# A gated attention and two feed-forward layers on one core: values loaded without padding, low weight parts of the first block on GpSimd, tiles 7 to 9 in three terms

## The chip, the core and the metric

One core of a Trainium2 chip runs the whole program. The time is device microseconds of one execution, and shorter is better. The kernel before takes 883.21 us (median of 3 runs, 882.9 to 884.86).

## What is computed

A gated linear attention over 4 batches, 8 heads, 768 tokens and 48 dimensions per head, whose output (3072 tokens of 384 values) goes through two feed-forward layers of width 2048:

```python
f = 1.0 / (1.0 + np.exp(-f_logit))
for t in range(S):
    state = f[:, :, t, :, None] * state + np.einsum('bhd,bhe->bhde', k[:, :, t], v[:, :, t])
    y[:, :, t] = np.einsum('bhd,bhde->bhe', q[:, :, t], state)
x = y.transpose(0, 2, 1, 3).reshape(B * S, H * D)
h = np.maximum(x @ w_in, 0.0);  x = h * h @ w_out            # first layer
h = x @ w_in2;  x = np.where(h > 0, h, np.exp(np.minimum(h, 0)) - 1) @ w_out2   # second layer
```

The weights are float64 in memory and q, k, v and the gates float32.

## The kernel before

The tokens are cut into 24 **chunks** of 128 (numbered g; one batch each, so chunks 0 to 3 begin the four batches), and four chunks make one **block** of 512 tokens. There are six blocks in the first layer and six in the second. A layer has 16 **weight tiles** f, each with an up half (384 to 128) and a down half (128 to 384). One pair (block, tile) is a **unit**; unit u's up product `ph` (line 475) stands in TensorE's queue ahead of the down product `y` (line 539) of unit u-2, and attention work of later chunks is set between them by the table `plan`, filled with `at(slot, f, ...)`: what is planned for slot u is written ahead of the up product of unit u.

A product of the first layer comes in two forms. **Three-term** splits both operands into a high part (rounded to fp32r) and a low part (the remainder) and adds high by high, low by high and high by low, three fp32r instructions per 128x128 block of weights. **One-term** multiplies fp32 as it is, two passes per block of weights. In block 0 the up products of tiles 0 to 2 (`DIRECT` = 3) and the down products of tiles 0 to 9 (`WHOLE` = 10) are one-term, everything else is three-term.

In block 0 the weights have to be made first. `load_raw` fetches the float64 tile; `begin_weights` (ScalarE, two instructions, lines 71 and 73) and `finish_weights` (VectorE, two instructions, lines 81 and 82) turn it into fp32 in a tile called `pair` or `dec`; `store_weights` allocates the lasting tile `w0_f` and, for a one-term tile, has a DMA copy the raw fp32 half into it; `split_up` makes the high part on ScalarE (line 435) and the low part on VectorE (line 436), of the up half alone where f < `WHOLE`, of both halves from there on. `split_rest` does the remaining halves in block 1. Tile f is begun at slot f-3, finished at f-2, split at f-1 and used by `up` at slot f. `between` evacuates `ph`: square of the ReLU, and for a three-term down product also the rounded `gh` (VectorE, line 502) and the remainder `gl` (VectorE in block 0, line 516; GpSimd later, line 522).

Per chunk VectorE runs `a_decay` (two scans, lines 182 and 184), `a_scale` (k and q times the decays, line 204), `a_mask` (two predicated copies out of PSUM, line 260) and `a_states` (lines 248 to 251); GpSimd runs half of the gate (`ff`, line 174), a small product `wc` (line 191) and a small copy into `ends` (line 194).

The opening, before slot 2, is a list written out by hand: `START`, one letter and number per step (f, q, v: loads; r: `load_raw`; g, d, c, s, t, k, m, y, x: attention of chunks 0 to 3; b, w, C, S: begin, finish, store, split; U, B: up and between). All loads go through SyncE's queue, in which each DMA also waits for the DMA eight places ahead of it. Values of chunks 0 to 3 come padded from memory: 128x672 (`vz`) instead of 128x384 (`vk`), so that the output of a head pair lands in the right rows.

Engines run their queues in order, and the order of all of it is the order in which the program writes it.

Of the kernel before, what the change touches and what calls it, by code (L numbers as in the profile page):

```python
# [11 lines left out]
F32 = mybir.dt.float32  # L12
# [5 lines left out]
AF = mybir.ActivationFunctionType  # L18
# [13 lines left out]
BLOCKS = [(layer, sum(n[:i]), n[i]) for layer, n in enumerate(SIZES) for i in range(len(n))]  # L32


START = """f0 f1 q0 I q1 M f2 v0 f3 v1 g0 q2 d0 q3 c0 g1 r0 d1 s0 W v2 c1 v3 t0 g2 k0 m0 g3 r1 s1 t1 y0 d2 c2
x0 r2 k1 m1 s2 d3 f4 q4 t2 y1 c3 b0 k2 s3 m2 x1 r3 t3 b1 y2 x2 m3 y3 x3 w0 k3 r4 b2 w1 U0 C0 r5 b3 w2 B0 h0 h1 w3 g4 h2 h3
f5 l0 l1 C1 U1 l2 l3 r6 C3 S3 B1 C2 T"""
STAGED = 27
DIRECT = 3
EARLY = 14  # L40
WHOLE = 10
NEAR = dict(zip(range(B, NG), (5, 8, 10, 12, 19, 21, 23, 25, *range(28, 4 * NG - 23, 4))))
ORDER = np.r_[64:128, 63:-1:-1]
DMIN = 2.0**-52
# [3 lines left out]
def at_(p, j):  # L48

    return j  # L50
# [31 lines left out]
    V.scalar_tensor_tensor(out=out, in0=hi, scalar=0x80000000, in1=out, op0=ALU.bitwise_and, op1=ALU.bitwise_or)  # L82


def chunked(ctx, tc, ff, qk, vk, vz, wraw, mask, ident, flag, out):

# [50 lines left out]
    def load_qk(g):  # L139
# [5 lines left out]
        else:  # L145
# [2 lines left out]
            nc.sync.dma_start(out=s["k"], in_=qk[g, :, 1])  # L148
            nc.sync.dma_start(out=s["q"], in_=qk[g, :, 0])

    def load_v(g):
        if g < B:

            if g % 2 == 0:
                t = two.tile([128, 2, NK, 2, 112], F32, tag=f"x{'hl'[g // 2]}", name=f"vz{g}")
                st["vz"] = t
            v = st["vz"][:, g % 2]
            nc.sync.dma_start(out=v.rearrange("r k j d -> r (k j d)"), in_=vz[g])
            st.setdefault(g, {})["vz"] = v
            return  # L160
        v = two.tile([128, NP, 2, 48], F32, tag="vk", name=f"vk{g}")
# [100 lines left out]
    def a_state(g):  # L262
        s = st[g]
        kvp = ps_a.tile([128, NP, 48], F32, tag="a0", name=f"kv{g}")
        for p in range(NP):
            for j, (lo, hi) in enumerate(((0, 64), (64, ROWS))):
                v = s["vz"][:, p, at_(p, j), 0:48] if p < NK else s["vz"][:, :, at_(p, j), 96:112]
                PE.matmul(kvp[lo:hi, p], s["kt"][:, p, lo:hi], v, start=True, stop=True)
        A.activation(state[g % B], kvp[:ROWS], AF.Copy)

    def a_direct(g):
# [67 lines left out]
    def a_whole(g):  # L339

        if g == 0:
            st["x"] = wpool.tile([128, NK, 512], F32, tag="w", name="x")
        A.activation(st["x"][:, :, 128 * g:128 * g + 128], st[g]["yp"], AF.Copy)

    def a_hi(g):
        i, o = where[g]
# [39 lines left out]
        raws[layer, f] = raw = pool.tile([128, 2 * DM], I64, tag=tag, name=f"raw{layer}_{f}")  # L386
        nc.sync.dma_start(out=raw, in_=wraw[layer, f])

    decs = {}

    def begin_weights(f):

# [7 lines left out]
        decs[f] = b  # L400

    def finish_weights(f):
        finish(nc, raws.pop((0, f)), decs[f])

    def store_weights(f):

        wt[0, f] = t = wpool.tile([128, 2, 2, DM], F32R, tag="w", name=f"w0_{f}")
        if f >= WHOLE:
            return
        t, b = t.bitcast(F32), decs[f].bitcast(F32)  # L410
        if f < DIRECT:
            nc.sync.dma_start(out=t[:, 1].rearrange("r i m -> r (i m)"), in_=b)
        else:
            nc.sync.dma_start(out=t[:, 1, 1], in_=b[:, DM:])

    def split_up(f):
        b = decs.pop(f).bitcast(F32)
        if f < WHOLE:
            split(wt[0, f][:, :, 0:1], b[:, :DM])
        else:  # L420
            split(wt[0, f], b)

    def split_rest(f):
        t = wt[0, f] if f < DIRECT else wt[0, f][:, :, 1:2]
# [101 lines left out]
    def down(i, f):  # L526
        layer, t0, n = BLOCKS[i]
        gh, gl, gg = hs.pop((i, f))
        if gh is None:
            terms = (wt[0, f][:, 1, 1].bitcast(F32), gg),  # L530
        else:
            w = wt[layer, f]
            terms = (w[:, 0, 1], gh), (w[:, 1, 1], gh), (w[:, 0, 1], gl)
        if f == 0:
            yp_[i] = [ps_y.tile([128, n], F32, tag=f"y{m}", name=f"y{i}_{m}") for m in range(NK)]
        for c in pieces(i, f):
            for m in range(NK):
                for n_, (w, b) in enumerate(terms):
                    PE.matmul(  # L539
                        yp_[i][m][:, c], w[:, 128 * m:128 * m + 128], b[:, c],  # L540
                        start=(f == 0 and n_ == 0), stop=(f == NF - 1 and n_ == len(terms) - 1),
                        skip_group_check=i == final[0],
                    )
            if f == NF - 1:
                dst = out if layer else x2d
                for m in range(NK):
                    if c.start == 0:
                        yo[m] = three.tile([128, n], F32, tag="yo", name=f"yo{i}_{m}")
                    y = yo[m][:, c]
                    if m % 2 == ((i, f) != final):  # L550
                        A.activation(y, yp_[i][m][:, c], AF.Copy)  # L551
                    else:
                        V.tensor_copy(y, yp_[i][m][:, c])
                    ends = (i, f) == final and m == NK - 1 and c.stop == n
                    (nc.scalar if ends else nc.sync).dma_start(out=dst[m, :, t0 + c.start:t0 + c.stop], in_=y)
# [61 lines left out]
    with tc.manual_schedule():  # L617
        V.memset(lim, DMIN)
        V.memset(ends[:, B], 1.0)
        V.memset(ss[0], 0.0)  # L620
        G.memset(ss[1], 0.0)
        for a in sd:
            G.memset(a, 0.0)

        def busy():
            again = ps_a.tile([128, 512], F32, tag="a1", name="busy")
            for _ in range(2):
                PE.matmul(again, idt, idt.unsqueeze(1).to_broadcast([128, 4, 128]), start=True, stop=True)

        warm = ps_a.tile([128, 512], F32, tag="a2", name="warm")  # L630
        for _ in range(3):
            PE.matmul(warm, ss[0][:, 0, 0], ss[0][:, 0].rearrange("r p t -> r (p t)"), start=True, stop=True)
        steps = {
            "I": lambda: nc.sync.dma_start(out=idt, in_=ident),
            "M": lambda: nc.sync.dma_start(out=msk, in_=mask),
            "T": lambda: [nc.sync.dma_start(out=tri[c:c + 64], in_=mask[c:c + 64, 64 - c:128 - c]) for c in (0, 64)],
            "f": load_f, "q": load_qk, "v": load_v, "r": lambda f: load_raw(0, f),
            "g": a_gate, "d": a_decay, "c": a_scale, "s": a_scores, "t": a_transposed, "m": a_mask, "k": a_state,
            "y": a_direct, "h": a_hi, "l": a_lo,
            "x": a_whole, "b": begin_weights, "w": finish_weights, "C": store_weights, "S": split_up, "W": busy,  # L640
            "U": lambda f: up(0, f), "B": lambda f: between(0, f),
            "L": lambda f: low(0, f),
        }
# [120 lines left out]


def _layout(q, k, v, f_logit, moe_w_in, moe_w_out, moe2_w_in, moe2_w_out):
# [14 lines left out]
    vz = np.zeros((B, 128, NK, 2, 112), v.dtype)
    vp = vk[:B].reshape(B, 128, NP, 2, D)
    for kk in range(NK):
        for j in range(2):
            vz[:, :, kk, j, :48] = vp[:, :, kk, at_(kk, j)]
            vz[:, :, kk, j, 96:] = vp[:, :, NK, at_(NK, j), 16 * kk:16 * kk + 16]
    vz = vz.reshape(B, 128, -1)
# [13 lines left out]
    for c, a in enumerate((f_logit, q, k, v)):  # L801
# [20 lines left out]
```

## Time and profile before

| | us |
|---|---|
| median of 3 runs | 883.21 |
| profiled execution | 885.04 |
| its span, first to last instruction | 883.2 |
| TensorE busy in the span | 868.0 |
| VectorE busy | 555.7 |
| ScalarE busy | 454.5 |
| GpSimd busy | 280.3 |

The page gives each engine's busy time; the chain of work that ended last is 94% TensorE. Inside the span the load changes by stage: up to about 37 us the opening, with DMAs at their limit; to about 110 us block 0 of the first layer, where the weights are made; then the blocks that only use them. So what the change does is read in the first 110 us. In a timeline row the columns are start, duration, engine, line, operation, output and input, shape, count, and in brackets how long the engine stood idle ahead of it and what ended that.

### The profile page before, as it was taken

The numbers are of one execution on the slowest core, as the hardware profiler recorded it, in microseconds if no ns is written. First come the engines' busy times: TensorE is split into PE (matmuls) and PEld (weight loads), VectorE is DVE, ScalarE is ACT, GpSimd is POOL, SyncE is SP. The second block draws the span as 40 slices with busy tenths as digits, with TensorE's granted clock in tenths as the row PEclk, the third lists the DMA queues.
The fourth block names the chain that finished last, engine by engine and source line by source line (L and its number), as shares of the span: only waits on it lengthen the run. The fifth ranks groups of instructions, "written<-read, shape, count | busy, mean of one in ns | idle before, by whom it ended". The sixth has DMA issues, their size and how long they took to land.

```text
span 883.2 us, 16000 instructions
## 1 busy us (share of the span) xinstructions
PE 868.0 (98%) x6262; PEld 701.1 (79%) x6262; DVE 555.7 (63%) x841; ACT 454.5 (51%) x812; POOL 280.3 (32%) x248
## 2 busy tenths in 40 slices
PE   7999999999999999999999999999999999999996
PEld 4566788888888888888888888888888888888885
DVE  8899796876778777644331655655654664564543
ACT  4778845555445555454554544544444444544443
POOL 2121065423333333323232333233332322322331
PEclk9999999999999999999999999999999999999998
DMA  8994232235434434422776300100100101000001
GB/s 268 345 301 138 57 108 87 84 115 184 153 121 151 151 117 152 150 77 107 252 275 224 131 13 1 66 6 11 62 1 27 46 1 39 33 1 37 1 1 39
DMA packets 35779, 91.22 MB, mean 103 GB/s; under 512 B 5728, under 2 KB 12352, under 8 KB 35696
## 3 DMA queue, kind: packets, MB, share of 16 engines
q1 hardware_dynamic: 35552, 90.00, 30.6%
q8 instruction: 50, 0.82, 0.4%
q14 instruction: 33, 0.27, 0.1%
q10 hardware_dynamic: 144, 0.13, 0.0%
HBM read 64.55 MB, written 22.02 MB: 98 GB/s over the span
## 4 chain that ended last, share of the span: by engine, by line
PE 94%; DMA 3%; DVE 1%; ACT 1%; SPq 0%; issue 0%; ACTq 0%; DVEq 0%
PE y L539 44%; PE ph L475 44%; DMA raw<-wraw 3%; PE o L294 1%; PE o L309 1%; PE tp L210 1%; PE sk_a L233 1%; DMA q<-qk 1%; PE sk_a L242 1%; PE sk_h L242 0%; PE sk_h L233 0%; DVE t L508 0%; SPq L136 0%; DVE xl L356 0%; DVE pair L81 0%
## 5 line engine op out<-in xcount | busy, mean ns | idle before, releaser
L522 POOL TENSOR_TENSOR gl<-gg,gh 128x512 fp32r<-128x512 f32 x175 | 234.5, 1340 | 452.6 <-PE ph L475 192.1
L539 PE MATMUL y<-gh,wf 128*128 128x512 f32 (+1 forms) x582 | 177.9, 387 | 0.3 <-ACT yo L551 0.3
L508 DVE SCALAR_TENSOR_TENSOR t<-r,t 128x512 f32<-128x512 f32 (+1 forms) x97 | 72.3, 745 | 154.6 <-ACT r L507 154.4
L539 PE MATMUL y<-gh,w 128*128 128x512 f32 x516 | 158.9, 389 | 0.0
L504 ACT ACTIVATE r<-ph 128x512 f32<-128x512 f32 (+1 forms) x97 | 57.8, 596 | 181.3 <-PE ph L475 176.4
L475 PE MATMUL ph<-xh,w 128*128 128x512 f32 x558 | 148.0, 400 | 0.0
L475 PE MATMUL ph<-xh,wf 128*128 128x512 f32 (+1 forms) x582 | 146.4, 387 | 0.0
L539 PEld LDWEIGHTS y<-gh,wf 128*128 128x128 f32 x582 | 108.8, 188 | 22.7 <-ACT yo L551 0.5
L475 PEld LDWEIGHTS ph<-xh,wf 128*128 128x128 f32 x582 | 108.6, 188 | 22.3
L475 PEld LDWEIGHTS ph<-xh,w 128*128 128x128 f32 x558 | 101.3, 188 | 22.1 <-issue 0.5
L539 PEld LDWEIGHTS y<-gh,w 128*128 128x128 f32 x516 | 96.9, 188 | 20.1
L539 PE MATMUL y<-gl,wf 128*128 128x512 f32 (+1 forms) x291 | 112.6, 387 | 0.0
L496 ACT ACTIVATE r<-ph 128x512 f32<-128x512 f32 x86 | 51.3, 596 | 104.2 <-PE ph L475 88.9
L539 PE MATMUL y<-gl,w 128*128 128x512 f32 x258 | 100.4, 389 | 0.0
L475 PE MATMUL ph<-xl,wf 128*128 128x512 f32 (+1 forms) x291 | 81.0, 387 | 0.0
L475 PE MATMUL ph<-xl,w 128*128 128x512 f32 x279 | 78.5, 390 | 0.0
L502 DVE TENSOR_TENSOR gh<-r 128x512 fp32r<-128x512 f32 x68 | 47.1, 693 | 44.4 <-ACT r L496 44.3
L509 DVE SCALAR_TENSOR_TENSOR gg<-ph,t 128x512 f32<-128x512 f32 (+1 forms) x97 | 66.6, 686 | 10.4 <-DVE t L508 0.5
L539 PEld LDWEIGHTS y<-gl,wf 128*128 128x128 f32 x291 | 54.6, 188 | 11.2
L475 PEld LDWEIGHTS ph<-xl,wf 128*128 128x128 f32 x291 | 54.3, 188 | 11.1
L506 ACT ACTIVATE t<-r 128x512 f32<-128x512 f32 (+1 forms) x97 | 61.1, 630 | 3.1
L507 ACT ACTIVATE r<-r 128x512 f32<-128x512 f32 (+1 forms) x97 | 61.0, 629 | 3.1
(112 smaller groups left out, 1027.2 us busy)
## 6 DMA issues: line engine op xcount, KB each, us to landing
raw<-wraw SPq DMA_DIRECT2D x32, 768.0 KB, 7.0
wst<-w SPq DMA_DIRECT2D x16, 768.0 KB, 3.3
wf<-wst SPq DMA_DIRECT2D x16, 768.0 KB, 4.7
k<-qk SPq DMA_DIRECT2D x22, 224.0 KB, 3.5
q<-qk SPq DMA_DIRECT2D x22, 224.0 KB, 4.6
ff<-ff SPq DMA_DIRECT2D x21, 227.9 KB, 6.6
x2d<-yo SPq DMA_DIRECT2D x18, 256.0 KB, 2.8
x<-x2d SPq DMA_DIRECT2D x18, 256.0 KB, 3.0
```

What stands on the lines that cost most here:

```text
L210: PE.transpose(tp[:, p, 0:ROWS], k[:, p], idt[:ROWS, :ROWS])
L233: PE.matmul(sc[j][64 * c:64 * c + 64, p], k[lo:hi, p, 64 * c:64 * c + 64], q[lo:hi, p, 64 - 64 * c:128 - 64 * c], start=True, stop=True,)
L475: PE.matmul(ph, w[:, a, 0, 128 * k:128 * k + 128], b[:, k, c], start=(m == 0), stop=(m == len(todo) - 1))
L496: A.activation(r[:, c], ph, AF.Relu)
L502: V.tensor_tensor(out=gh[:, c], in0=r[:, c], in1=r[:, c], op=ALU.mult)
L504: A.activation(r[:, c], ph, AF.Relu, scale=-1.0)
L506: A.activation(t[:, c], r[:, c], AF.Tanh, scale=-0.5)
L507: A.activation(r[:, c], r[:, c], AF.Exp, scale=-1.0)
L508: V.scalar_tensor_tensor(out=t[:, c], in0=r[:, c], scalar=1.0, in1=t[:, c], op0=ALU.add, op1=ALU.mult)
L509: V.scalar_tensor_tensor(out=gg[:, c], in0=ph, scalar=0.0, in1=t[:, c], op0=ALU.max, op1=ALU.add)
L522: G.tensor_tensor(out=gl, in0=gg, in1=gh, op=ALU.subtract)
L539: PE.matmul(yp_[i][m][:, c], w[:, 128 * m:128 * m + 128], b[:, c], start=(f == 0 and n_ == 0), stop=(f == NF - 1 and n_ == len(terms) - 1) ...
```

## The change

- Values of chunks 0 to 3 are loaded as 128x384 like all others. `kv` (line 268) reads them directly; a new step `a_padded` (letter z) copies them on ScalarE, two instructions per chunk, into padded tiles whose gaps GpSimd zeroes once, for the product `yp`.
- In `START`, `f4`, `r4`, `q4` and others stand elsewhere: the raw tiles 3 and 4 are loaded ahead of k and q of chunk 4, and the gate of chunk 4 comes last.
- The fp32 weights of tile 0 are finished in halves, and the last quarter of x is copied in three pieces.
- The one-term down products of tiles 0 to 2 read the fp32 `pair` tile instead of the copy that the DMA makes.
- `split_up` makes high and low part one half at a time, and the low part on GpSimd for tiles 4 to 15; tile 3 stays on VectorE.
- `WHOLE` goes from 10 to 7: the down products of tiles 7 to 9 in block 0 become three-term. They need `gh` and `gl`, their down halves are split at once, and their raw copies and their `split_rest` fall away.

```diff
-x0 r2 k1 m1 s2 d3 f4 q4 t2 y1 c3 b0 k2 s3 m2 x1 r3 t3 b1 y2 x2 m3 y3 x3 w0 k3 r4 b2 w1 U0 C0 r5 b3 w2 B0 h0 h1 w3 g4 h2 h3
-f5 l0 l1 C1 U1 l2 l3 r6 C3 S3 B1 C2 T"""
+x0 r2 k1 m1 s2 d3 t2 z2 y1 c3 b0 z3 k2 s3 m2 x1 r3 f4 r4 q4 t3 b1 y2 x2 m3 y3 x3 w0 k3 b2 w1 U0 r5 b3 C0 w2 U1 B0 h0 h1 w3 C1 h2 h3
+f5 r6 l0 l1 C3 S3 l2 l3 B1 g4 C2 T"""
...
-WHOLE = 10
+WHOLE = 7
...
+    def a_padded(g):
+        v, z = st[g]["vk"], padded[g // 2][:, g % 2]
+        A.activation(z[:, :, :, 0:48], v[:, :NK], AF.Copy)
+        A.activation(z[:, :, :, 96:112], v[:, NK].rearrange("r j (k d) -> r k j d", k=NK), AF.Copy)
+        st[g]["vz"] = z
...
-        A.activation(st["x"][:, :, 128 * g:128 * g + 128], st[g]["yp"], AF.Copy)
+        for k in [slice(k, k + 1) for k in range(NK)] if g == B - 1 else [slice(0, NK)]:
+            A.activation(st["x"][:, k, 128 * g:128 * g + 128], st[g]["yp"][:, k], AF.Copy)
...
-        finish(nc, raws.pop((0, f)), decs[f])
+        raw = raws.pop((0, f))
+        for c in (slice(0, DM), slice(DM, 2 * DM)) if f == 0 else (slice(0, 2 * DM),):
+            finish(nc, raw[:, c], decs[f][:, c])
...
     def split_up(f):
         b = decs.pop(f).bitcast(F32)
-        if f < WHOLE:
-            split(wt[0, f][:, :, 0:1], b[:, :DM])
-        else:
-            split(wt[0, f], b)
+        t = wt[0, f]
+        for i in range(1 if f < WHOLE else 2):
+            A.activation(t[:, 0, i], b[:, DM * i:DM * i + DM], AF.Copy)
+        for i in range(1 if f < WHOLE else 2):
+            E = G if f > DIRECT else V
+            E.tensor_tensor(out=t[:, 1, i], in0=b[:, DM * i:DM * i + DM], in1=t[:, 0, i], op=ALU.subtract)
```

The first place is GpSimd's queue in block 0. `ff` is the gate, `wc` and `ends` belong to a chunk's decays, `w0_f` is the lasting weight tile f. Before:

```order
L174 TENSOR_SCALAR ff6_530<-ff6_530 112x521
L191 TENSOR_TENSOR wc6_674<-ds0_90,ends_88 112x4
L194 COPY ends_88<-ds0_90 112x8
L174 TENSOR_SCALAR ff7_634<-ff7_634 112x521
L191 TENSOR_TENSOR wc7_841<-ds1_91,ends_88 112x4
L194 COPY ends_88<-ds1_91 112x8
```

and now:

```order
L180 TENSOR_SCALAR ff6_548<-ff6_548 112x521
L432 TENSOR_TENSOR w0_7_654<-pair6_509,w0_7_654 128x384 x2
L197 TENSOR_TENSOR wc6_693<-ds0_90,ends_88 112x4
L200 COPY ends_88<-ds0_90 112x8
L432 TENSOR_TENSOR w0_8_697<-pair8_624,w0_8_697 128x384 x2
L180 TENSOR_SCALAR ff7_652<-ff7_652 112x521
L432 TENSOR_TENSOR w0_9_819<-pair8_624,w0_9_819 128x384 x2
L197 TENSOR_TENSOR wc7_870<-ds1_91,ends_88 112x4
L200 COPY ends_88<-ds1_91 112x8
L432 TENSOR_TENSOR w0_10_874<-pair10_704,w0_10_874 128x384 x2
L432 TENSOR_TENSOR w0_11_996<-pair10_704,w0_11_996 128x384 x2
```

The low parts of tiles 4 to 15 now stand in this queue (one instruction each for tiles 4 to 6, two each for 7 to 15), that of tile 10 behind `wc7` and `ends7`; in the same way that of tile 4 stands behind the gate `ff5` and that of tile 5 behind `ends5`.

The second place is VectorE's queue around tile 9, before (`pair` tiles are weights being finished, `sd`, `s0`, `s1` and `state` belong to a chunk's states):

```order
L436 TENSOR_TENSOR w0_8_678<-pair8_606,w0_8_678 128x384
L81 SCALAR_TENSOR_TENSOR pair8_606<-pair8_606,raw0_9_511 128x768
L82 SCALAR_TENSOR_TENSOR pair8_606<-raw0_9_511,pair8_606 128x768
L260 COPY_PREDICATED sd1_96<-tri_92,sk5_a2_727 128x256
L260 COPY_PREDICATED sd1_96<-tri_92,sk5_h_728 128x256
L248 TENSOR_TENSOR s0_97<-state1_100,wc5_524 112x192
```

and now:

```order
L81 SCALAR_TENSOR_TENSOR pair8_624<-pair8_624,raw0_9_529 128x768
L82 SCALAR_TENSOR_TENSOR pair8_624<-raw0_9_529,pair8_624 128x768
L513 TENSOR_TENSOR gh0_7_720<-r0_7_722 128x512
L527 TENSOR_TENSOR gl0_7_721<-gg0_7_723,gh0_7_720 128x512
L266 COPY_PREDICATED sd1_96<-tri_92,sk5_a2_751 128x256
L266 COPY_PREDICATED sd1_96<-tri_92,sk5_h_752 128x256
L254 TENSOR_TENSOR s0_97<-state1_100,wc5_542 112x192
```

A low part leaves VectorE's queue per tile (tiles 4 to 15), and `gh` and `gl` of tiles 7, 8 and 9 enter it.

The third place is SyncE's queue in the opening, before:

```order
L387 DMA raw0_1_206<-wraw 128x768
L387 DMA raw0_2_247<-wraw 128x768
L136 DMA ff4_281<-ff 112x521
L148 DMA k4_284<-qk 112x512
L149 DMA q4_283<-qk 112x512
L387 DMA raw0_3_335<-wraw 128x768
L387 DMA raw0_4_383<-wraw 128x768
```

and now:

```order
L393 DMA raw0_1_214<-wraw 128x768
L393 DMA raw0_2_257<-wraw 128x768
L393 DMA raw0_3_343<-wraw 128x768
L136 DMA ff4_345<-ff 112x521
L393 DMA raw0_4_347<-wraw 128x768
L148 DMA k4_350<-qk 112x512
L149 DMA q4_349<-qk 112x512
```

Raw tile 3 moved ahead of three loads of chunk 4.

## Rows read from the trace of the kernel before

**Rows 1.** Stretches: length, busy us (count) by engine, granted clock, DMA share, GB/s.
```profile
20.00:30.00 10.00, 8.51 (x118) 6.65 (x115) 8.99 (x12) 6.93 (x12) 0.00 (x0) 1.00 1.04 336
...
36.00:110.00 74.00, 73.92 (x748) 49.68 (x747) 65.97 (x105) 60.60 (x111) 11.08 (x13) 1.00 0.59 187
```

**Rows 2.** Timeline of TensorE at the end of the opening.
```profile
34.36 2.84 PE L464 MATMUL ph<-x,pair 128*128 128x512 f32 x6 [1.24 <-ACT r L484]
37.28 2.84 PE L539 MATMUL y<-gg,w 128*128 128x512 f32 x6
```

**Rows 3.** Timeline of ScalarE there: raw tile 3 has landed.
```profile
32.16 0.90 ACT L71 ACTIVATE pair<-raw 128x768 f32<-128x768 f32 x1 [2.56 <-DMA raw<-wraw]
```

**Rows 4.** Timeline of VectorE there.
```profile
24.18 1.36 DVE L260 COPY_PREDICATED ss<-msk,sc 128x512 f32<-128x512 int32 x2 [0.51 <-PE sc L220]
...
33.85 0.96 DVE L81 SCALAR_TENSOR_TENSOR pair<-pair,raw 128x768 uint32<-128x768 uint32 x1 [2.28 <-ACT raw L73]
...
35.72 1.97 DVE L356 TENSOR_TENSOR xl<-yp,xh 128x384 fp32r<-128x384 f32 x4
```

**Rows 5.** The chain that ended last, in block 0: start, us, what.
```profile
74.72 2.57 PE y L539 x6
...
79.26 2.27 PE ph L475 x9
...
98.32 2.05 PE y L539 x9
...
105.31 2.04 PE ph L475 x9
```

**Rows 6.** Timeline of VectorE in slots 2 and 3: scans, finish, scale, low part.
```profile
38.11 0.07 DVE L180 MEMSET lim<- 112x9 f32 x1
...
41.01 0.95 DVE L81 SCALAR_TENSOR_TENSOR pair<-pair,raw 128x768 uint32<-128x768 uint32 x1
...
42.88 0.68 DVE L204 TENSOR_TENSOR k<-k,ds 112x512 f32<-112x512 f32 x1
...
44.08 0.55 DVE L436 TENSOR_TENSOR w<-pair,w 128x384 fp32r<-128x384 f32 x1
```

**Rows 7.** Timeline of VectorE in slots 9 to 12: low part, masks and states, gh and gl.
```profile
75.62 0.95 DVE L436 TENSOR_TENSOR w<-pair,w 128x768 fp32r<-128x768 f32 x1
...
78.86 0.45 DVE L260 COPY_PREDICATED sd<-tri,sk_a 128x256 f32<-128x256 int32 x1 [0.42 <-PE sk_h L242]
...
79.53 0.35 DVE L248 TENSOR_TENSOR s<-state,wc 112x192 f32<-112x192 f32 x1
...
80.59 0.68 DVE L204 TENSOR_TENSOR k<-k,ds 112x512 f32<-112x512 f32 x1
...
84.54 0.68 DVE L502 TENSOR_TENSOR gh<-r 128x512 fp32r<-128x512 f32 x1
...
85.93 0.55 DVE L358 TENSOR_TENSOR xl<-x,xh 128x384 fp32r<-128x384 f32 x1
```

**Rows 8.** All instructions of two GpSimd lines: ns min/median/max, first and last start.
```profile
L522 POOL TENSOR_TENSOR gl<-gg,gh x175: 1275/1308/2302, 115.0 to 868.5; 128x512 fp32r<-128x512 f32 x175
...
L174 POOL TENSOR_SCALAR ff<-ff x20: 626/643/2477, 36.3 to 352.4; 112x521 f32<-112x521 f32 x20
```

**Rows 9.** Timeline of VectorE in block 1 of the first layer.
```profile
160.83 0.55 DVE L358 TENSOR_TENSOR xl<-x,xh 128x384 fp32r<-128x384 f32 x1
161.29 1.96 DVE L204 TENSOR_TENSOR k<-k,ds 112x512 f32<-112x512 f32 x1
...
169.96 0.45 DVE L260 COPY_PREDICATED sd<-tri,sk_a 128x256 f32<-128x256 int32 x1 [0.37 <-PE sk_h L242]
```

**Rows 10.** Timeline of GpSimd in slot 9 and in block 1.
```profile
75.84 1.66 POOL L194 COPY ends<-ds 112x8 f32<-112x8 f32 x1 [1.43 <-DVE ends L193]
...
161.40 1.31 POOL L522 TENSOR_TENSOR gl<-gg,gh 128x512 fp32r<-128x512 f32 x1
...
169.61 1.30 POOL L522 TENSOR_TENSOR gl<-gg,gh 128x512 fp32r<-128x512 f32 x1
```

More of the change, by code (lines that the diff above doesn't have):

```diff
@@ L32 @@
 BLOCKS = [(layer, sum(n[:i]), n[i]) for layer, n in enumerate(SIZES) for i in range(len(n))]
-START = """f0 f1 q0 I q1 M f2 v0 f3 v1 g0 q2 d0 q3 c0 g1 r0 d1 s0 W v2 c1 v3 t0 g2 k0 m0 g3 r1 s1 t1 y0 d2 c2
-x0 r2 k1 m1 s2 d3 f4 q4 t2 y1 c3 b0 k2 s3 m2 x1 r3 t3 b1 y2 x2 m3 y3 x3 w0 k3 r4 b2 w1 U0 C0 r5 b3 w2 B0 h0 h1 w3 g4 h2 h3
-f5 l0 l1 C1 U1 l2 l3 r6 C3 S3 B1 C2 T"""
+START = """f0 f1 q0 I q1 M f2 v0 f3 v1 g0 q2 d0 q3 c0 g1 r0 d1 s0 W v2 c1 v3 t0 g2 z0 k0 m0 g3 r1 s1 t1 z1 y0 d2 c2
+x0 r2 k1 m1 s2 d3 t2 z2 y1 c3 b0 z3 k2 s3 m2 x1 r3 f4 r4 q4 t3 b1 y2 x2 m3 y3 x3 w0 k3 b2 w1 U0 r5 b3 C0 w2 U1 B0 h0 h1 w3 C1 h2 h3
+f5 r6 l0 l1 C3 S3 l2 l3 B1 g4 C2 T"""
 STAGED = 27
@@ L82, in finish, with chunked @@
     V.scalar_tensor_tensor(out=out, in0=hi, scalar=0x80000000, in1=out, op0=ALU.bitwise_and, op1=ALU.bitwise_or)
-def chunked(ctx, tc, ff, qk, vk, vz, wraw, mask, ident, flag, out):
+def chunked(ctx, tc, ff, qk, vk, wraw, mask, ident, flag, out):
     nc = tc.nc
@@ L149, in load_qk @@
             nc.sync.dma_start(out=s["q"], in_=qk[g, :, 0])
+    padded = []
     def load_v(g):
[L152 to L161, printed above, removed]
+        if g == 0:
+            for p in "hl":
+                z = two.tile([128, 2, NK, 2, 112], F32, tag=f"x{p}", name=f"vz{p}")
+                G.memset(z[:, :, :, :, 48:96], 0.0)
+                padded.append(z)
+        v = (two if g < 2 or g >= B else three).tile(
+            [128, NP, 2, 48], F32, tag="vk" if g < 2 or g >= B else "yo", name=f"vk{g}"
+        )
         nc.sync.dma_start(out=v.rearrange("r p j d -> r (p j d)"), in_=vk[g])
         st.setdefault(g, {})["vk"] = v
+    def a_padded(g):
[3 more added lines that the diff above has]
+        st[g]["vz"] = z
     def a_gate(g):
@@ L266, in a_state @@
             for j, (lo, hi) in enumerate(((0, 64), (64, ROWS))):
-                v = s["vz"][:, p, at_(p, j), 0:48] if p < NK else s["vz"][:, :, at_(p, j), 96:112]
-                PE.matmul(kvp[lo:hi, p], s["kt"][:, p, lo:hi], v, start=True, stop=True)
+                PE.matmul(kvp[lo:hi, p], s["kt"][:, p, lo:hi], s["vk"][:, p, at_(p, j)], start=True, stop=True)
         A.activation(state[g % B], kvp[:ROWS], AF.Copy)
@@ L387, in load_raw @@
         nc.sync.dma_start(out=raw, in_=wraw[layer, f])
-    decs = {}
+    decs, whole = {}, {}
     def begin_weights(f):
@@ L411, in store_weights @@
         if f < DIRECT:
+            whole[f] = decs[f]
             nc.sync.dma_start(out=t[:, 1].rearrange("r i m -> r (i m)"), in_=b)
@@ L529, in down @@
         if gh is None:
-            terms = (wt[0, f][:, 1, 1].bitcast(F32), gg),
+            w = whole[f][:, DM:] if f < DIRECT else wt[0, f][:, 1, 1]
+            terms = (w.bitcast(F32), gg),
         else:
@@ L638, in chunked @@
             "g": a_gate, "d": a_decay, "c": a_scale, "s": a_scores, "t": a_transposed, "m": a_mask, "k": a_state,
-            "y": a_direct, "h": a_hi, "l": a_lo,
+            "y": a_direct, "z": a_padded, "h": a_hi, "l": a_lo,
             "x": a_whole, "b": begin_weights, "w": finish_weights, "C": store_weights, "S": split_up, "W": busy,
@@ L754, in gated_attention_moe @@
 @with_exitstack
-def gated_attention_moe(ctx: ExitStack, tc: tile.TileContext, ff, qk, vk, vz, nat, wraw, mask, ident, out):
+def gated_attention_moe(ctx: ExitStack, tc: tile.TileContext, ff, qk, vk, nat, wraw, mask, ident, out):
     pool = ctx.enter_context(tc.tile_pool(name="flag", bufs=1))
@@ L758, in gated_attention_moe @@
     with ExitStack() as inner:
-        chunked(inner, tc, ff, qk, vk, vz, wraw, mask, ident, flag, out)
+        chunked(inner, tc, ff, qk, vk, wraw, mask, ident, flag, out)
     rv = tc.nc.values_load(flag[0:1, 0:1], min_val=0, max_val=1)
@@ L780, in _layout @@
     vk = v.reshape(B, NP, 2, NC, 128, D)[:, :, :, :, outward].transpose(3, 0, 4, 1, 2, 5).reshape(NG, 128, DM)
[L781 to L787, printed above, removed]
     rows = []
@@ L805, in _layout @@
     return {
-        "ff": ff, "qk": qk, "vk": vk, "vz": vz, "nat": nat, "wraw": wraw, "mask": mask,
+        "ff": ff, "qk": qk, "vk": vk, "nat": nat, "wraw": wraw, "mask": mask,
         "ident": np.eye(128, dtype=np.float32),
```

## The prediction

> **What bounds the kernel now.** I read the stretches first, then the end of the opening and the chain in block 0, then VectorE and GpSimd instruction by instruction. From 36 to 110 us TensorE is busy 73.92 of 74 us at granted clock 1.00, the higher level [rows 1]. The chain there is its own matmuls [rows 5]. So a microsecond is won only if TensorE starts that stretch earlier or has less work, and lost as soon as anything makes it wait. Behind it stands VectorE, busy 65.97 of the same 74 us [rows 1], which makes the weights that TensorE uses one slot later. Its room is small: tile 10's low part ends at 76.57 and TensorE wants it at about 79.3 [rows 5, 7]. The opening is different: VectorE idles 0.51 for scores and 2.28 for raw tile 3, which lands at 32.16 [rows 3, 4]; behind it wait ScalarE's evacuation for the third `ph` (1.24 us of TensorE idle) and the `xl` that free the PSUM banks of the first `y` at 37.28 [rows 2, 4].
>
> **Opening.** Ahead of raw tile 3 go four times 144 KB of padding and three loads of chunk 4 (228, 224, 224 KB): 1.28 MB, at 336 GB/s 3.8 us [rows 1], so it lands near 28.3 instead of 32.16. VectorE gets back 2.28 and, since the value loads are small, the 0.51 of rows 4. It pays for tile 0 in halves (four instructions of about 0.55 for two of 0.95: 0.3), for the low part of tile 3, now ahead of the third `xl` (0.47, the step from 44.08 to the next start being its 0.55 less overlap), and some 0.2 waiting for that high part: 2.8 - 1.0 = **1.8 us**; the first `y` starts at 35.5. Not seen: the eight padding copies on ScalarE. By share of the 0.90 for 768 elements [rows 3] they are 0.34 and 0.11 each, at most 0.9; some 2 us, covered by ScalarE's idle (6.93 of 10 busy [rows 1]). Should ScalarE not have that room, the gain falls to nothing, so its bounds are 0 and 2.8. The two memsets, the raw copy no longer read by the first `y` and the three pieces of x sit off this path: 0.
>
> **Three terms.** A one-term down product takes 2.57, a three-term one 2.05 [rows 5]: three tiles give 3 x 0.52 = **1.6 us** of TensorE work. If nothing else happened, `ph` of tile 15 would start at 105.31 - 1.8 - 1.6 = 101.9. The later `split_rest` of tiles 7 to 9 goes too, at a time when VectorE isn't waited for: 0.
>
> **Low parts on GpSimd.** VectorE loses six low parts of a half (0.47 each) and six of a whole tile (0.87): 8.0 us. It gains `gh` and `gl` of three tiles, 1.39 each (84.54 to 85.93 [rows 7]): 4.2. By itself that is relief. But GpSimd's work is not beside VectorE's. At 161.40 GpSimd starts a subtraction of 1.31, and VectorE's product k, started at 161.29, lasts 1.96 where the same instruction takes 0.68 elsewhere: 1.28 longer, all of GpSimd's time [rows 6, 9, 10]. The predicated copies, which take data from PSUM, keep their 0.45 beside such a subtraction [rows 9, 10]. So with two SBUF inputs the engines take turns. A low part of 384 columns is not in the trace; by share of the 1.275 for 512 [rows 8] it is 0.96. Its bounds are VectorE's own 0.55 [rows 6] and the whole 1.28. I take 0.96, the same instruction on the same engine.
>
> The sum for the turn-taking pair runs from chunk 4's first scan (36.95: `xl` end at 36.0, and the gate of chunk 4, now last in the opening, about one later) to the low part of tile 15's up half. VectorE: four scan blocks of 2.90 (38.11 to 41.01), twelve finishes of 1.87 (41.01 to 42.88), four pairs of k and q of 1.20 (42.88 to 44.08) [rows 6]; four blocks of masks and states of 1.73 (78.86 to 80.59), `gh` and `gl` six times 1.39 and one `gh` of 0.7, two `xl` of 0.47 [rows 7]. That is 11.6 + 22.4 + 4.8 + 6.9 + 9.0 + 0.9 = 55.6. GpSimd: three low parts for tiles 4 to 6, sixteen for 7 to 14, one for 15, 20 x 0.96 = 19.2; three gates of 0.63 [rows 8], 1.9. Together 76.7. GpSimd can work beside VectorE in the PSUM parts, masks 0.67 and two state sums about 0.67 per block: 5.4 in four. Walking through both queues I find a low part ready in two of three such places: 3.6. So 36.95 + 76.7 - 3.6 = 110.05.
>
> TensorE's first matmul of tile 15 needs only the high part; the second needs this low part, 0.23 later: `ph` starts at 109.9, not 105.31. **Forecast: +4.6 us**, a gain of 3.4 turned over by stalls of 8.0. The same sum up to tile 10's low part: 36.5 of VectorE, 11.5 of GpSimd, 1.8 covered, 83.2. GpSimd's order alone would allow no better, since that low part stands behind `wc7` and `ends7`, which wait for VectorE's scans, and the copy there took 1.66 [rows 10]. So `ph` of tile 10 starts near 83, not 79.26. Smaller waits come at tile 4 (behind the gate of chunk 5, 1 us), tile 5 (behind `ends5`, 2 us) and near tile 13, where the far product waits for chunk 7's states. Queued behind the late low parts are only further low parts; behind the late finishes stand ScalarE's high parts and with them its evacuations, which have a slot to spare. From block 1 on VectorE has room, TensorE is the chain again, and nothing is given back.
>
> The Trainium skill, GPSIMD Engine Reference, section Engine selection, puts a two-input operation on GpSimd at about twice VectorE's time. By an estimate from that page a low part would be 1.1, and the 20 of them 2.8 us more: 890.6. Rows 8 and 7 put the ratio for 512 columns a little lower (1.275 against 0.68), so I stay with the row.
>
> **Against the runs.** The profiled execution took 885.04 with a span of 883.2, 1.84 of it outside. It gives 885.04 + 4.6 = 889.6. The median lies 1.83 below, so 883.21 + 4.6 = **887.8**.
>
> **Rivals.** (1) *The low parts fit, and the kernel is faster.* VectorE has 8.0 idle us in the stretch [rows 1], loses 8.0 and gains 4.2 of work: 11.8 free, less 3.4 by which TensorE's stretch shortens, plus 5.4 beside PSUM work: 13.8. Twenty low parts fit if one holds the other engine for 13.8 / 20 = 0.69 or less. That is the point of decision, between VectorE's 0.55 and my 0.96. Then waits at tiles 4 and 5 of about 1.0 in all remain: 883.21 - 3.4 + 1.0 = 880.8. For it: VectorE's pauses for ScalarE would be filled. Against: k's 1.96 in rows 9. (2) *Nearly even.* All 5.4 are covered (1.8 better), the opening gives all 2.8 (1.0 better), and gates hold VectorE 0.3 instead of 0.63 (1.0 better): +0.8, 884.0. (3) *Raw tile 3 is not earlier*, because each load waits for the one eight places ahead or ScalarE's copies are in the way: the 1.8 is gone and everything shifts, 889.6; the move in the opening then doesn't do what its order says. (4) *No cover at all*: +8.2, 891.4, on the forecast's side.
>
> **How the numbers follow.** Forecast 0.50 (886 to 890.5), rival 1 0.23, rival 2 0.15, rival 3 0.05, rival 4 0.07. The unknown costs are the opening (0 to 2.8) and a low part (0.55 to 1.28: 20 x 0.41 less, 20 x 0.32 more); the cheap end is rival 1. The range 880.2 to 891.5 holds them but for the ends of rivals 1 and 4. Where the forecast's side alone counts, it is 885.0 to 891.5. A measurement can tell about 0.2% from no change, 1.8 us: faster than 881.4 is most of rival 1 (0.22), within is rival 2 with an edge of the others (0.14), slower is the rest (0.64).
>
> **What would show it.** Opening: the first `y` near 35.5 and no wait of VectorE for raw tile 3; if it stays at 37.3, rival 3. Low parts on GpSimd of 0.96 and up to 1.9 when they wait; VectorE's finish and scale instructions, 0.95 and 0.68 before, stretched to 1.6 to 1.9 between 43 and 108. TensorE waiting for GpSimd's weights at tiles 4, 5 and 10 and for VectorE's states near tile 13, 8 us in all; `ph` of tile 10 near 83 and of tile 15 near 109.9. The forecast is wrong if TensorE keeps its solid stretch: then either a low part is cheaper than 0.69, or VectorE and GpSimd find more than 3.6 us of cover, and VectorE's busy time between 36 and 110 would fall by about 4 instead of rising.

## The result, and the profile after

| | before | after |
|---|---|---|
| median, us (5 runs each) | 883.24 (882.9 to 884.86) | 888.23 (887.68 to 889.22) |
| profiled execution, us | 885.04 | 889.22 |
| its span, us | 883.2 | 887.4 |

The changed kernel takes 1.0055 of the time before, 95% interval [1.0044, 1.0066]: 5.0 us longer by the medians, 4.2 by the profiled executions. All of it arises before 110 us; from there on the gap between the two traces stays.

The opening did what it was made for. Timeline of TensorE at its end, to be read beside [rows 2]:

```profile
26.76 7.99 PE L475 MATMUL ph<-x,pair 128*128 128x512 f32 x18
34.76 2.81 PE L551 MATMUL y<-gg,pair 128*128 128x512 f32 x6
```

The three `ph` run without a break and the first `y` starts at 34.76 instead of 37.28, 2.5 us earlier. In VectorE's timeline the finish instructions of tile 3, which waited 2.28 us for raw tile 3 in [rows 4], now start without a wait:

```profile
30.78 0.95 DVE L81 SCALAR_TENSOR_TENSOR pair<-pair,raw 128x768 uint32<-128x768 uint32 x1
```

Then the stretches (length, busy us and count by engine, granted clock, DMA share, GB/s), beside [rows 1]:

```profile
36.00:110.00 74.00, 68.62 (x734) 48.28 (x733) 70.84 (x88) 55.66 (x107) 32.26 (x32) 0.98 0.50 158
...
86.00:88.00 2.00, 1.08 (x7) 1.03 (x8) 2.00 (x4) 0.72 (x2) 0.00 (x0) 1.00 0.00 0
88.00:90.00 2.00, 2.00 (x7) 1.54 (x6) 1.86 (x4) 0.70 (x3) 0.02 (x1) 0.57 0.00 0
90.00:92.00 2.00, 2.00 (x7) 1.57 (x6) 2.00 (x2) 2.00 (x4) 2.00 (x2) 0.57 0.01 4
```

TensorE, busy 73.92 of 74 us before, now stands idle 5.4 of them. VectorE's busy time went up by 4.9 although its work went down (8.0 us of low parts gone, 4.2 us of `gh` and `gl` added). The waits of TensorE in its timeline, all five:

```profile
49.83 0.50 PE L486 MATMUL ph<-xh,w 128*128 128x512 f32 x1 [1.04 <-POOL w L432]
71.78 0.57 PE L216 MATMUL tp<-idt,k 112*128 112x112 f32 x4 [0.74 <-issue]
78.15 0.72 PE L314 MATMUL o<-sd,vk 64*48 64x64 f32 x32 [0.17 <-ACT seen L306]
80.41 1.45 PE L486 MATMUL ph<-xh,w 128*128 128x512 f32 x5 [1.11 <-POOL w L432]
86.92 0.57 PE L216 MATMUL tp<-idt,k 112*128 112x112 f32 x4 [2.32 <-issue]
```

Two are for low parts from GpSimd (tiles 5 and 10, 2.15 us together). Two, 3.06 us together, are transposes of keys: `tp` at 71.78 starts just after VectorE's scaled k of chunk 6, `tp` at 86.92 just after that of chunk 7 (both below). Why VectorE is late is seen where its rows lie beside GpSimd's. GpSimd, then VectorE, in three places:

```profile
48.79 0.99 POOL L432 TENSOR_TENSOR w<-pair,w 128x384 fp32r<-128x384 f32 x1
...
68.56 0.63 POOL L180 TENSOR_SCALAR ff<-ff 112x521 f32<-112x521 f32 x1 [3.80 <-ACT ff L179]
69.16 1.97 POOL L432 TENSOR_TENSOR w<-pair,w 128x384 fp32r<-128x384 f32 x2
...
79.37 1.96 POOL L432 TENSOR_TENSOR w<-pair,w 128x384 fp32r<-128x384 f32 x2
82.78 2.44 POOL L432 TENSOR_TENSOR w<-pair,w 128x384 fp32r<-128x384 f32 x2 [1.45 <-ACT w L429]
```

```profile
48.81 1.78 DVE L82 SCALAR_TENSOR_TENSOR pair<-raw,pair 128x768 uint32<-128x768 uint32 x1
...
68.62 3.06 DVE L210 TENSOR_TENSOR k<-k,ds 112x512 f32<-112x512 f32 x1
...
79.39 2.75 DVE L82 SCALAR_TENSOR_TENSOR pair<-raw,pair 128x768 uint32<-128x768 uint32 x1
82.07 0.68 DVE L513 TENSOR_TENSOR gh<-r 128x512 fp32r<-128x512 f32 x1
82.85 1.50 DVE L527 TENSOR_TENSOR gl<-gg,gh 128x512 fp32r<-128x512 f32 x1
...
86.14 0.68 DVE L210 TENSOR_TENSOR k<-k,ds 112x512 f32<-112x512 f32 x1
```

A low part of 384 columns takes 0.99 us where it got there first. The instruction of VectorE that starts 0.02 us behind it takes 1.78 instead of its usual 0.96. Behind two low parts in a row (79.37) it takes 2.75, and the k of chunk 6, behind a gate and two low parts, 3.06 instead of 0.68. The Trainium skill ("SBUF — State Buffer", section "SBUF: two separate sides") says that the pair of SBUF ports that VectorE and GpSimd share goes to whichever instruction starts first, for the whole of it, and that the other blocks. These rows agree. Whether VectorE gets in between two queued instructions of GpSimd differs: at 69.16 and 79.37 its waiting instruction didn't, at 82.78 it did (`gl` takes 1.50, against 0.69 in the trace with all low parts on VectorE, below, and the two low parts 2.44 instead of 1.96). What decides that, these rows don't show.

The chain that ended last shows the wait for chunk 7's keys ("issue"), and what came of it (start, us, what), beside [rows 5]:

```profile
84.62 2.30 issue
86.92 0.57 PE tp L216 x4
87.50 3.08 PE ph L486 x9
90.57 2.65 PE y L551 x9
...
109.38 2.04 PE ph L486 x9
```

The products right behind that wait take 3.08 and 2.65 instead of 2.10 and 2.05: some 1.6 us more, in the stretches where the granted clock stands at 0.57 (at 0.50, the lower of its levels, 1.2 GHz, from 89 to 91 us). `ph` of tile 15 starts at 109.38, 4.07 later than in [rows 5].

The account by the traces: the opening gives 2.5, the three tiles 1.6 (`y` takes 2.05 in them); TensorE's idle time costs 5.4 and the clock 1.6. That makes +2.9 of the 4.07. The other 1.2 lies in the same places: with the wait of 1.04 us, the step from one `y` to the next (44.56 to 51.78) is 1.29 longer than in the trace with the opening alone, below (44.79 to 50.72), 0.25 more than the idle time. Counted in the same way, the steps between the `y` of tiles 6 to 9 (68.30, 74.27, 82.39 and 90.37, there 67.23, 72.28, 79.09 and 84.14) are 0.2, 0.55 and 0.15 longer than their idle time, the clock's 1.0 and the 0.5 saved by each three-term product explain. So a wait here costs more than the idle time that it shows; why, no row shows.

### The profile page after: what moved, and what is told of

Read it like the earlier page. It is cut to its first block, busy times and chain, and to the rows that moved or that the text cites. A ratio compares the mean times of both kernels' runs of the same rounds, so it can differ in the third digit from the quotient of the medians.

```text
span 887.4 us, 16062 instructions
## 1 busy us (share of the span) xinstructions
PE 868.3 (98%) x6271; PEld 704.6 (79%) x6271; DVE 564.7 (64%) x834; ACT 456.5 (51%) x828; POOL 302.3 (34%) x271
## 4 chain that ended last, share of the span: by engine, by line
PE 90%; DVE 5%; ACT 2%; DMA 1%; issue 1%; POOL 1%; DVEq 0%; ACTq 0%; POOLq 0%
PE ph L486 42%; PE y L551 42%; DMA ff<-ff 1%; PE o L299 1%; PE o L314 1%; DVE ds L188 1%; PE tp L216 1%; DVE pair L82 1%; PE sk_a L239 1%; DVE ds L190 1%; DVE pair L81 1%; DVE k L210 1%; PE yp L283 0%; PE sk_a L248 0%; PE sk_h L248 0%
## 5 line engine op out<-in xcount | busy, mean ns | idle before, releaser
L551 PE MATMUL y<-gh,w 128*128 128x512 f32 x534 | 165.1, 391 | 0.0
L551 PEld LDWEIGHTS y<-gh,w 128*128 128x128 f32 x534 | 100.7, 189 | 21.1
L551 PE MATMUL y<-gl,w 128*128 128x512 f32 x267 | 104.3, 390 | 0.0
```

Source lines behind the costliest of these rows:

```text
L551: PE.matmul(yp_[i][m][:, c], w[:, 128 * m:128 * m + 128], b[:, c], start=(f == 0 and n_ == 0), stop=(f == NF - 1 and n_ == len(terms) - 1) ...
```

## The experiments

Three of the change's parts can be set separately: the opening, the three-term tiles 7 to 9 (`WHOLE`), and the engine of the low parts (E). All runs are stated against runs of the kernel before on the same chip (medians 883.4 to 883.7), and a difference in us is one of medians.

**Do turns between GpSimd and VectorE cost time by themselves?** The kernel before, with 18 subtractions of 384 columns added to GpSimd that nobody reads.

```diff
+        for i in range(0 if f <= DIRECT else 1 if f < WHOLE else 2):
+            hi = wt[0, f][:, 0, i].bitcast(F32)
+            G.tensor_tensor(out=idle, in0=hi, in1=hi, op=ALU.subtract)
```

> The kernel before, with nothing moved: GpSimd makes 18 extra subtractions of 384 columns in block 0, one beside each low part of tiles 4 to 9 and two beside those of tiles 10 to 15, from a high part with itself into a scratch tile that nothing reads. No engine waits for them by data. Theory (VectorE and GpSimd take turns): 18 x 0.96 = 17.3 us of GpSimd, less 3.6 beside PSUM work, lands on VectorE, which has 8.0 idle us in the stretch 36 to 110 and about 2.7 of lead: TensorE is held up, 886 to 889 us, and VectorE's busy time in the stretch goes from 66 to 71 or more. Rival (the low parts are late only because of where they stand in GpSimd's queue): nobody waits for these, so 883.2 us and VectorE stays at 66.

Measured: 887.63 us, ratio 1.0044 [1.003, 1.0057], +3.9. VectorE is busy 71.59 of the 74 us, as expected, and waits nowhere in them for GpSimd. In the timelines GpSimd's subtraction lies beside the finish instruction of VectorE:

```profile
52.08 0.82 POOL L425 TENSOR_TENSOR idle<-w 128x384 f32<-128x384 f32 x1
```

```profile
52.09 1.62 DVE L82 SCALAR_TENSOR_TENSOR pair<-raw,pair 128x768 uint32<-128x768 uint32 x1
...
56.54 0.55 DVE L440 TENSOR_TENSOR w<-pair,w 128x384 fp32r<-128x384 f32 x1
```

After the opening TensorE waited only for VectorE's low parts (2.1 us in three places), which by data have nothing to do with the added work:

```profile
57.15 1.43 PE L479 MATMUL ph<-xh,w 128*128 128x512 f32 x5 [0.99 <-DVE w L440]
...
104.17 1.42 PE L479 MATMUL ph<-xh,w 128*128 128x512 f32 x5 [0.69 <-DVE w L440]
...
108.96 1.43 PE L479 MATMUL ph<-xh,w 128*128 128x512 f32 x5 [0.40 <-DVE w L440]
```

From the first `y` (37.45) to that of tile 13 (110.90) it takes 73.5 us, before 69.9 (37.28 to 107.19). So work that is useless to everyone, put on an engine that stood idle most of the time, costs the kernel 3.9 us through VectorE. The turns are shown.

**The low parts alone.** The kernel before, with `split_up` as after (tile 4 on).

```diff
-            split(wt[0, f][:, :, 0:1], b[:, :DM])
...
+            E = G if f > DIRECT else V
+            E.tensor_tensor(out=t[:, 1, i], in0=b[:, DM * i:DM * i + DM], in1=t[:, 0, i], op=ALU.subtract)
```

> The kernel before with only the low parts of tiles 4 to 15 on GpSimd (halves one at a time, as in the changed kernel). Theory (turns): 8.0 us leave VectorE, 17.3 of GpSimd come, 3.6 covered: 5.7 more for the pair, against 8.0 idle and 2.7 of lead; with waits at tiles 4, 5 and 10 about 885 to 886 us. Rival (three-term tiles are the cause): VectorE is relieved, 883 us or a little less.

Measured: 885.26, ratio 1.002 [1.0011, 1.0029], +1.6, as the theory had it. One wait of 1.12 us for a low part (tile 4, behind the gate of chunk 5) is all that TensorE shows after the opening; the expectation had waits at tiles 5 and 10 as well.

**All low parts back on VectorE.** The changed kernel with one word changed.

```diff
-            E = G if f > DIRECT else V
+            E = V
```

> The changed kernel with all low parts of block 0 on VectorE, everything else kept. Theory (turns): VectorE has 55.6 + 20 x 0.47 = 65.0 us from the first scan of chunk 4 at 36.0 on, gates 1.9, so the up product of tile 15 starts near 102.7 instead of 109.4 and the kernel takes about 880.6 to 881.5 us. Rival (the gh and gl of tiles 7 to 9 overload VectorE, whoever makes the low parts): VectorE is fuller than in the changed kernel, 888 us or more.

Measured: 884.82, ratio 1.0012 [1.0003, 1.0021], +1.1. Neither held: 3.9 us of the loss go away, but 3.3 to 4.2 more that the theory promised do not come. Timeline of TensorE, then of VectorE:

```profile
83.01 0.57 PE L216 MATMUL tp<-idt,k 112*128 112x112 f32 x4 [1.95 <-issue]
```

```profile
79.11 0.69 DVE L513 TENSOR_TENSOR gh<-r 128x512 fp32r<-128x512 f32 x1
79.90 0.69 DVE L527 TENSOR_TENSOR gl<-gg,gh 128x512 fp32r<-128x512 f32 x1
...
82.23 0.68 DVE L210 TENSOR_TENSOR k<-k,ds 112x512 f32<-112x512 f32 x1
```

The wait for chunk 7's keys is there without GpSimd: the scaled k stands in VectorE's queue behind `gh` and `gl` of tile 9, which the three-term form added. VectorE as a whole is idle for 4.7 of the 74 us (69.27 busy), but not here.

**The opening alone.** The changed kernel with E = V and two terms back for tiles 7 to 9 (`WHOLE = 10`).

> The changed kernel with the low parts on VectorE and ten one-term tiles as before: what is left is the opening, the values without padding and the order of the loads. Theory: the first down product starts at 34.8 instead of 37.3 and VectorE keeps up, 880.7 us. Rival: VectorE can't follow a TensorE that starts 2.5 us earlier, since its own chunk 4 starts only 2.3 earlier and its slack was under 1 us at tiles 4 to 6, and the gain is taken back there: 882.5 to 883.2 us.

Measured: 882.5, ratio 0.9984 [0.9975, 0.9993], -1.2; TensorE is busy 74.00 of 74 us in the stretch. The time is the rival's, but its mechanism isn't there, since TensorE doesn't wait. The profiled executions differ by more: the span is 880.5 against 883.2, and `ph` of tile 15 starts at 103.04, 2.3 earlier than in [rows 5]. The profiled execution of before lay 1.8 above its median and this one at its median. Three more kernels of this section have the old opening, and their traces show why (us):

| old opening, in the trace of | ScalarE begins raw tile 3 | VectorE's wait for it | first `y` |
|---|---|---|---|
| the kernel before | 32.16 | 2.28 | 37.28 |
| the useless subtractions | 32.31 | 1.91 | 37.45 |
| the low parts alone | 30.52 | 1.68 | 35.66 |
| three terms alone (below) | 29.63 | 0.68 | 34.79 |

Raw tile 3 lands at a different time in each, and the first `y` follows it by 5.1 to 5.2 us. In the eight traces with the new opening the first `y` starts at 34.68 to 35.38. So the trace of before is that of a late execution, and the 2.5 us are measured against that one; by the medians the opening gives 1.2. What the new opening takes away is mostly a spread: the runs of before on this chip lie between 883.0 and 885.5, those with the opening alone between 882.2 and 882.8.

**Two terms, low parts on GpSimd.** The changed kernel with `WHOLE = 10`. (The expectation counts the low parts too low: there are 18 of them here, and 21 in the changed kernel.)

> The changed kernel with tiles 7 to 9 back on two terms: the new opening and the low parts on GpSimd (14 of 384 columns for tiles 4 to 13 instead of 17), no added products by VectorE. Theory (turns between VectorE and GpSimd are what costs, and the costs add): the low parts alone cost the kernel before 1.6 us (885.26 against 883.7), the opening alone gave 1.2 to 2.7, so 882.5 to 884.0; no wait of TensorE for a low part over 0.6 us. Rival (the three-term tiles have no part in the loss; the earlier start alone brings TensorE to the low parts too soon): 886 or more, with the 1 us waits at tiles 5 and 10 still there.

Measured: 884.04, ratio 1.0003 [0.9994, 1.0012], +0.6, just outside the upper end of the theory; one wait of 1.03 us at tile 5, where the theory allowed none over 0.6, and none at tile 10. It is far from the rival's 886.

**Three terms alone.** The kernel before with `WHOLE = 7`.

```diff
-WHOLE = 10
+WHOLE = 7
```

> The kernel before with nothing but tiles 7 to 9 on three terms, all low parts on VectorE. Theory (three-term tiles take 1.6 us of TensorE but give VectorE six subtractions more of products and weights, about 3 x (0.68 + 0.68 + 0.55) = 5.7 us in a stage with 8 us to spare, and in the changed opening the same step cost 2.3 us): a loss of 0 to 2.5 us, 883.5 to 886. Rival (the step costs only because the earlier start of TensorE leaves VectorE less time; in the old opening the 2.5 us are there): 882.0 to 882.6, TensorE's own saving of 1.6 us kept whole.

Measured: 885.68, ratio 1.0028 [1.0019, 1.0036], +2.2. A step that takes 1.6 us from TensorE lengthens the kernel by 2.2, without GpSimd and without the new opening. The traced execution happens to start early (first `y` at 34.79), but none of the 11 runs (885.09 to 887.76) keeps the saving, as the rival had it. TensorE's timeline has the wait for chunk 7's keys, and the clock falls behind it here as well (stretches below it):

```profile
82.71 0.57 PE L210 MATMUL tp<-idt,k 112*128 112x112 f32 x4 [1.45 <-issue]
84.13 2.50 PE L475 MATMUL ph<-xh,w 128*128 128x512 f32 x5 [0.60 <-DVE w L436]
```

```profile
84.00:86.00 2.00, 1.87 (x4) 1.50 (x5) 1.97 (x4) 0.03 (x1) 0.00 (x0) 0.54 0.00 0
86.00:88.00 2.00, 2.00 (x7) 1.63 (x6) 1.90 (x4) 2.00 (x3) 0.00 (x0) 0.61 0.00 0
```

**Only the low parts of the down halves on GpSimd.** The changed kernel with the engine chosen by the half (9 low parts on GpSimd, where the expectation says 7, of 21).

```diff
-            E = G if f > DIRECT else V
+            E = G if i else V
```

> The changed kernel with the low parts of the up halves back on VectorE; those of the down halves, which are needed one slot later, stay on GpSimd (7 of them instead of 17). Theory (what GpSimd takes from VectorE is time of the pair's turns, in proportion to how many parts it does and worst for two in a row): between the kernel with all of them on VectorE (884.8) and the changed one (888.2), nearer the first: 884 to 886, no VectorE instruction of 384 columns over 2.0 us. Rival (what counts is that the down halves of tiles 7 to 9 land in the same slots as the scaled keys of chunks 6 and 7, on whichever engine): 887 or more, with TensorE still waiting over 1.5 us for the keys of chunk 7.

Measured: 886.45, ratio 1.0033 [1.002, 1.0046], +3.0: between the two numbers, so neither theory is clean. No instruction of VectorE took over 1.81 us, as the first had it. But the wait that the rival named is there, longer than ever (2.44 us, for chunk 7's keys), with the clock at 0.58 behind it:

```profile
84.23 0.92 PE L216 MATMUL tp<-idt,k 112*128 112x112 f32 x4 [2.44 <-issue]
```

There one low part alone, which made the finish instruction ahead of `gh` and `gl` take 1.81 us instead of 0.96, was added to the products.

**The rounded square on ScalarE.** If `gh` of tiles 7 to 9 is what makes the keys late, it can be moved: ScalarE makes this square for later tiles anyway. First with all low parts on VectorE.

```diff
-                if i == n1 - 1 or (i == 0 and f >= EARLY):
+                if i == n1 - 1 or (i == 0 and (f >= EARLY or f < 10)):
```

> All low parts on VectorE, and the rounded square of tiles 7 to 9 by ScalarE instead of VectorE (3 x 0.68 us off VectorE, 3 x 0.62 us on ScalarE). Theory (with all low parts on VectorE the loss against the opening alone, 884.8 against 882.5, is VectorE's: the keys of chunk 7 are scaled 1.95 us late): the 2 us taken off VectorE end that wait, and 881.0 to 882.5 results, below the kernel with the new opening alone. Rival (ScalarE has no room either: 0.62 us more in each of these slots delays the squares, and TensorE waits for the products instead): 884 to 885.5.

Measured: 882.58, ratio 0.9988 [0.9979, 0.9997], -0.9. The wait for the keys is gone, 2.0 us by the medians. It is also no better than the opening alone: TensorE waits twice for ScalarE (`o` for `seen`, 0.60 as in the run with all low parts on VectorE, and 0.26 that is new), and the steps at these tiles are longer by the whole of the 1.6 us that TensorE should save. The idle time alone is 0.9 of it. Then with the low parts on GpSimd, as in the changed kernel:

> The changed kernel as it is, low parts on GpSimd, but the rounded square of tiles 7 to 9 on ScalarE. Theory (two separate losses: VectorE's added products make the keys of chunk 7 late, 2.3 us, and the clock falls behind that wait, 1.6 us; the low parts on GpSimd make the weights late at tiles 5 and 10, 2.1 us, with or without the square): the wait for the keys falls under 0.8 us, the granted clock of 36 to 110 us returns to 1.00, the waits of 1 us for low parts stay: 884 to 885.5. Rival (the low parts alone hold VectorE so long that the keys of chunk 7 are late anyway): 886.5 or more, with over 1.5 us of wait for the keys.

Measured: 884.86, ratio 1.0015 [1.0006, 1.0024], +1.2, in the theory's range, 3.8 less than the changed kernel. The wait for the keys is 0.98 us (a little over the 0.8 expected), the clock of the stretch is back at 1.00, and the wait for the low part of tile 5 is still there; that of tile 10, which the theory kept, is not, and one of 0.58 for ScalarE (`o` for `seen`) has come:

```profile
36.00:110.00 74.00, 71.22 (x753) 50.88 (x752) 71.86 (x90) 61.06 (x116) 32.79 (x33) 1.00 0.54 170
```

```profile
49.77 1.43 PE L486 MATMUL ph<-xh,w 128*128 128x512 f32 x5 [1.03 <-POOL w L432]
...
83.78 0.57 PE L216 MATMUL tp<-idt,k 112*128 112x112 f32 x4 [0.98 <-PE y L551]
```

**A version that beats both.** The new opening, all low parts on VectorE, and only tile 9 on three terms (`WHOLE = 9`), its square on ScalarE.

> The new opening, all low parts on VectorE, and only tile 9 on three terms, with its rounded square on ScalarE. Theory (three terms are worth 0.52 us each where VectorE has room, and the three tiles together cost as much as they saved): no TensorE wait over 0.3 us, 882.0 to 882.4, 0.1 to 0.5 under the kernel with the new opening alone (882.5). Rival (already one more low part and one more product by VectorE in that slot brings a wait as long as what is saved): 882.5 to 883.

Measured: 881.86, ratio 0.9978 [0.9969, 0.9987], -1.9, 0.14 under the theory's range; TensorE has no wait in the stretch (74.00 of 74 busy):

```profile
36.00:110.00 74.00, 74.00 (x759) 51.74 (x758) 67.77 (x111) 60.58 (x115) 9.20 (x13) 1.00 0.55 172
```

Side by side, differences of medians to the kernel before:

| opening | three terms | low parts on | us |
|---|---|---|---|
| old | no | GpSimd | +1.6 |
| old | tiles 7 to 9 | VectorE | +2.2 |
| new | no | VectorE | -1.2 |
| new | no | GpSimd | +0.6 |
| new | tiles 7 to 9 | VectorE | +1.1 |
| new | tiles 7 to 9 | down halves: GpSimd | +3.0 |
| new | tiles 7 to 9 | GpSimd (the change) | +5.0 |
| new | tiles 7 to 9, square on ScalarE | VectorE | -0.9 |
| new | tiles 7 to 9, square on ScalarE | GpSimd | +1.2 |
| new | tile 9, square on ScalarE | VectorE | -1.9 |

Moving the low parts to GpSimd costs 1.6 to 2.1 wherever `gh` of tiles 7 to 9 isn't on VectorE (in this table row 1; row 4 less 3; row 9 less 8). Three terms with `gh` on VectorE cost 2.2 to 2.3 wherever the low parts aren't on GpSimd (row 2; row 5 less 3). Both together cost 6.2 (row 7 less 3), some 2.1 more than the sum, and the trace of after shows where: the finish instruction held for 2.75 us and, behind it, `gh` and a `gl` that was held too stand ahead of the same scaled key, and the clock falls once that wait is long.

## Why the prediction was right

**The time** (887.8, and 888.23 came) and the mechanism of the turns held: GpSimd and VectorE take turns, and useless subtractions at +3.9 show it. The stalls come to 7.8 us by the medians (5.0 lost, with 1.2 from the opening and 1.6 from the three tiles gained), against 8.0. But the low parts on GpSimd account for only half of them: 3.9 (1.1, 1.2 and 1.6) are there with all low parts on VectorE.

**Opening.** 1.8 was predicted and 2.5 came in the profiled execution, inside the bounds of 0 to 2.8: raw tile 3 came early enough, and the padding copies (0.43 and 0.27 for a chunk, against 0.34 and 0.11 estimated) found room on ScalarE. By the medians it is 1.2: the 1.8 was worked out from an execution in which raw tile 3 came late (the table above) and then set against the median. Rival 3 is out.

**Price of a low part.** 0.96 by share of [rows 8], 0.98 to 1.0 unhindered in the trace. So the 0.69 from which rival 1 decides wasn't met, and rival 1 is out. What the prediction missed is that two in a row hold VectorE for both: it looked for VectorE instructions of 1.6 to 1.9, and there are some of 2.75 and 3.06.

**The sum.** `ph` of tile 15 was put at 109.9 and starts at 109.38. On the way it is less exact. The up half's low part of tile 10 was to be ready at 83.2 and TensorE got it at 80.41, so that the sum ran 2.8 us late at that point; of the 2.3 us by which the rest of TensorE's way was longer than worked out, the fallen clock explains 1.6. Nor is the end of the sum what `ph` of tile 15 waited for. The low part of tile 15's up half ends at 108.68 (against 110.05), before that `ph` starts:

```profile
107.28 1.40 POOL L432 TENSOR_TENSOR w<-dec,w 128x384 fp32r<-128x384 f32 x1 [2.72 <-ACT w L429]
```

From 87.50 on the chain that ended last is TensorE's own products, slowed by the clock. Part of the agreement at the end is therefore luck.

**Places of the waits.** Idle time of 5.4 us came instead of 8. Right: tiles 5 (1.04 instead of 2) and 10 (1.11). Wrong: none at tile 4, none near tile 13. Not foreseen: the keys of chunks 6 and 7, at 3.06 us the larger half of all idle time. The prediction listed k and q among VectorE's work, but didn't ask who waits for k: the transposes, which stand in TensorE's queue ahead of a `ph`.

**Three terms: this step failed.** It was booked at 1.6 us won, with the 4.2 us of products a "relief" for VectorE, since they are less than the low parts taken from it. The runs put it at 2.2 lost in the old opening and 2.3 in the new. The reckoning took VectorE's room as one sum over 74 us, and rival 1 and the 880.6 to 881.5 for the low parts back on VectorE rest on the same reckoning. But `gh` and `gl` of tile 9 land right ahead of chunk 7's states and key, in the one slot that has no room. So of the 5.0 us, the low parts weren't the only cause: with them back on VectorE the kernel still lost 1.1, where 2.2 to 3.1 won were expected.

**The clock** wasn't in the sum: 1.6 us.

## What to carry to other kernels

Before work goes to GpSimd because it is idle, look whether VectorE's instructions there read two inputs from SBUF and GpSimd's read SBUF too (the gate, with one input, held k as well); then its time is VectorE's time, and two instructions in a row can count as one long one. An engine's free time in a stretch says little about an instruction that is added there: list what stands behind it in the queue, and for each of those ask who waits for it. A saving on the bounding engine is worth having only where the helper engines of that slot have room, so it is taken tile by tile: one three-term tile won where three had won nothing.

## What the runs showed of the hardware

**A wait that costs more than its length.** Behind the wait of 2.32 us the granted clock was 0.57 in the two stretches from 88 to 92 us, and the two products there took 1.6 us more. The same came behind waits of 1.45 and, in the product right behind it, 0.60 (0.54 and 0.61 from 84 to 88, three terms alone) and of 2.44 (down halves on GpSimd). It did not come behind the 1.95 (and 0.21 in the product behind it) with all low parts on VectorE, where the stretch kept 1.00, nor behind any wait of 1.12 or less that stood alone. What decides between 1.95 + 0.21 and 1.45 + 0.60 these runs don't show.

**Useless work on an idle engine.** Eighteen subtractions whose result nobody reads, on an engine busy for 11 of 74 us, made the kernel 3.9 us longer. That is more than moving the same number of low parts there (1.6), since VectorE keeps its own.
